# The feed-forward part of a fused attention and mixture kernel on one core: its order written out by hand, the conversion of its weights changed

## The chip, the cores and the metric

The kernel runs on one core of a Trainium2 chip. The time is device time in microseconds for one execution. The engines are PE (TensorE; PEld is its loading of weights), DVE (VectorE), ACT (ScalarE), POOL (GpSimd) and SP, which here issues the DMAs. Each runs its own instructions in its own order and waits for others by semaphores.

## What is computed

Attention with a top-32 mask (4 batches, 8 heads, 576 positions), a soft mixture of 8 experts over its result, and a feed-forward layer over the 2304 tokens. The part that this document is on is the last:

```python
def _moe2_ref(x, w_in, w_out):          # w_in 512 x 2048, w_out 2048 x 512
    h = x @ w_in
    pos, neg = h >= 1.0, h <= -1.0
    g = np.where(pos, h, np.where(neg, 0.0, (h + 1.0) ** 2 / 4.0))
    return (g @ w_out).astype(np.float32)
```

The weights `w_in` and `w_out` come as float64, as pairs of 32-bit words, and the kernel turns them into float32 with integer and float instructions: the absolute value of the high word read as a float, a lower bound, a shift left by 3, plus the scaled low word, and the sign put back.

## The kernel before

The attention and the mixture stand first (to about 575 us of the span) and aren't touched. Then SP streams the weights of the experts, four pieces of `w_in` that are converted earlier, and the 16 raw tiles of `w_out` (128 rows, 512 KB each) through a ring of 37 tiles of SBUF. The order of these loads is the list `worder`; `NRAW` of the raw tiles stand ahead of the pieces for `m_rest`.

x is a product itself, c times the experts' result, so the kernel first makes m = (experts' result) @ w_in, in four parts m4[0..3] of 512 columns: `m_first` makes the first, `m_rest` the other three in 24 matmuls, `m_spread(n)` brings each of these into the form that the h matmul needs. The tokens are cut into 6 blocks t of 384, the 2048 hidden columns into 16 pieces f of 128. A step is one pair (t, f): `emit_g` makes h = m4 . c in one matmul into PSUM, then relu and square on ACT, min and max in one DVE instruction (called min below), and cuts the result g into a high half gh (a cast) and a low half gl (a subtraction). `emit_o` multiplies: for each of three rows of 128 tokens gh . wh, gh . wl, gl . wh, nine matmuls that add into PSUM. wh and wl are the same two halves of the converted `w_out` piece f.

The steps run as (0,0), (1,0), (0,1), (1,1), ... through all f for t = 0 and 1, and then t = 2 to 5 one after the other. `wo_prep(f)` converts piece f by `narrow` (seven instructions: abs, scaled low word and sign on ACT, shift on DVE, max, add and multiplication by the sign on POOL) and cuts it; it does so `CLA` = 4 pieces ahead. h is made `GA` = 2 steps ahead. In this part the order on each engine isn't the order of the code: the scheduler of the framework sets it by its own estimates. The attention's order is written by hand (`ORDER`, under `tc.manual_schedule`).

Of the kernel before, what the change touches and what calls it, by code (L numbers as in the profile page):

```python
# [19 lines left out]
P = 128  # L20
# [10 lines left out]
NF = DFF // P  # L31
# [7 lines left out]
NTILE = NPAIR * 9  # L39
BIG = 2.0 ** 100  # L40
NEG = -1.0e30
CW = 512
NC1 = DFF // CW
NC2 = DM // CW
NWE = 0
NRAW = 2
NCV = NHP * NC1 + NWE
BLK = 384
NA = 13
# [4 lines left out]
MASK_POOL = ((0, 1), (2, 1), (4, 0))  # L54
NTR = 1
NV = 2
CLA = 4
ORDER = '''
Y30b z4b E00b Q30c A11c X21b P11b T40c S00a md M31b H1c A20c Y21b Q31c K20b c4c U01b E01b C00a
G00a K21b K30b c2c L4b S01a Q40c U11b N3b C01a R4c X31b Y31b A21c E10b S10a T00b T01b G01a B2b  # L60
# [8 lines left out]
GA = 2  # L69
NLAST = 3  # L70
# [3 lines left out]
def kernel_body(tc, qT, kT, vP, phi, w1, w2, w_in, w_out, out, fast, flag):  # L74
    nc = tc.nc
# [25 lines left out]
    two = cpool.tile([P, 1], F32, name="two")  # L101
# [736 lines left out]
    def m_first():  # L838
        ps = ps_m.tile([P, 512], F32, name="m_ps0", tag="m_ps")
        for c in range(NHP):  # L840
            nc.tensor.matmul(ps, so128[:, c].rearrange("p g s -> p (g s)"), wtile[(2, 0, c // 2)][c % 2],
                             start=(c == 0), stop=(c == NHP - 1))
        nc.scalar.copy(m4[0], ps)
        nc.vector.tensor_tensor(m4[0][64:], ps[64:], m4[0][64:].bitcast(F32), op=ALU.subtract)

    def m_rest():
        ps = ps_m.tile([P, 512], F32, name="m_ps1", tag="m_ps")
        for c in range(NHP):
            for n in range(1, NC1):
# [30 lines left out]
    pos = {}  # L880
    wo_t = {}

    def wo_prep(f):
        if f < NWE:
            wo = wtile[(3, 0, f // 2)][f % 2]
        else:
            tr = p_t.tile([P, 2, CW], I32, name="tr_l", tag="h1s", bufs=2)
            sg = p_t.tile([P, CW], BF16, name="sg_l", tag="sg_l", bufs=1)
            wo = narrow(wtile[(4, 0, f)], tr, sg, range(7))
        wh, wl = slot_tiles(w_slots[f], "whl", F32R)[1]  # L890
        nc.scalar.copy(wh, wo)
        nc.vector.tensor_tensor(wl, wo, wh.bitcast(F32), op=ALU.subtract)
        wo_t[f] = (wh, wl)

    def emit_g(s_):
        t, f = s_
        ph = ps_m.tile([P, 512], F32, name="h_ps", tag="m_ps")[:, :BLK]
        nc.tensor.matmul(ph, m4[f // 4][:, f % 4 * P:(f % 4 + 1) * P], cT[:, t * BLK:(t + 1) * BLK], start=True, stop=True)  # L898
        r, g = (x[:, :BLK] for x in ring_tile("g", g_slots, "rg", F32))
        nc.scalar.activation(r, ph, AF.Relu, bias=half, scale=0.5)  # L900
        nc.scalar.activation(r, r, AF.Square)  # L901
        nc.vector.scalar_tensor_tensor(g, ph, 1.0, r, op0=ALU.max, op1=ALU.min)  # L902
        gh, gl = (x[:, :BLK] for x in ring_tile("g", g_slots, "ghl", F32R))
# [19 lines left out]
    m_first()
    for k in range(CLA):
        wo_prep(k)
    for s_ in steps[:GA]:
        emit_g(s_)
    for i, s_ in enumerate(steps[:-NLAST]):
        t, f = s_
        if i == 1:  # L930
            mhl = m_rest()
        if t == 1 and f % 4 == 1 and f // 4 < NC1 - 1:
            m_spread(f // 4 + 1, *mhl)
        if t == 0 and f + CLA < NF:
            wo_prep(f + CLA)
        if i + GA < len(steps):
            emit_g(steps[i + GA])
        emit_o(t, f, range(NS))
    for s_ in steps[GA - NLAST:] if NLAST > GA else []:
        emit_g(s_)  # L940
    for n in range(NS):
        for s_ in steps[-NLAST:]:
            emit_o(*s_, [n])
# [65 lines left out]
```

## Time and profile before

| | us |
|---|---|
| median of 3 runs | 877.66 (876.0 to 878.2) |
| span of the profiled execution | 872.0 |
| feed-forward steps of t = 0 and 1 (with conversion) | 634.2 to about 722 |
| steps of t = 2 to 5 (no conversion) | about 722 to 865 |

The span is that of the instructions which the profiler recorded; the time of a run has a few microseconds around it. Busy time of an engine is the time in which it had an instruction under way, waits inside an instruction included. A row of the timeline gives start, duration, engine, line, operation, and what it writes and reads; a line number with L is that of the listing.

### The profile page before, as it was taken

The page shows a single profiled execution, that of the slowest core. Times are in us where ns is not written, and L with a number is a line of the kernel's source. Part 1 is how long each engine was busy: PE and PEld are TensorE (multiplying, and loading weights), DVE is VectorE, ACT ScalarE, POOL GpSimd, SP SyncE. Part 2 cuts the span into 40 slices and gives each one's busy share as a digit, 9 for nine tenths or more (in the row PEclk, how much of TensorE's full clock was granted, in tenths as well). Part 3 has the DMA queues.
Part 4 walks back from the last instruction along what each step waited for, and adds up shares of the span by engine and source line. Part 5 has one row for each costly group of instructions (what it writes and reads, how often), then busy time and mean ns, then how long its engine had stood idle before and what let it go on. Part 6 is the DMA issues. An engine that isn't in the chain of part 4 may idle for free.

```text
span 872.0 us, 17711 instructions
## 1 busy us (share of the span) xinstructions
PE 821.5 (94%) x5695; PEld 674.7 (77%) x5695; DVE 685.8 (79%) x3084; ACT 644.8 (74%) x1292; POOL 485.4 (56%) x494
## 2 busy tenths in 40 slices
PE   4889999999999999999999999799698899999996
PEld 3678989988989988988988988632266678888885
DVE  6999999988999989999989994103389995666663
ACT  5688999988998988998988987412578766545453
POOL 2577888877888877888877774100467740000000
PEclk9799999999999999999999999899799999999999
DMA  8453563553353353353452536699940001001001
GB/s 240 124 152 96 165 176 98 156 157 89 103 142 92 112 133 89 102 142 87 117 134 78 157 101 205 206 343 386 399 175 1 0 2 73 37 0 38 1 37 40
DMA packets 49461, 108.59 MB, mean 125 GB/s; under 512 B 8304, under 2 KB 8304, under 8 KB 49360
## 3 DMA queue, kind: packets, MB, share of 16 engines
q1 hardware_dynamic: 49040, 106.73, 40.2%
q8 instruction: 47, 0.77, 0.4%
q10 hardware_dynamic: 320, 0.66, 0.3%
q14 instruction: 54, 0.44, 0.2%
HBM read 70.70 MB, written 8.91 MB: 91 GB/s over the span
## 4 chain that ended last, share of the span: by engine, by line
PE 78%; DVE 10%; DMA 6%; ACT 3%; POOL 1%; issue 1%; ACTq 0%; POOLq 0%; SPq 0%; DVEq 0%
PE s_ps L311 20%; PE o_ps L916 17%; PE av_ps L485 14%; PE pt_ps L457 7%; PE s_ps L413 4%; PE av_ps L486 3%; PE rem_ps L230 3%; DMA w<-in_moe_w_dram 2%; DMA w<-in_moe_w_out_dram 2%; PE h L804 2%; DVE cand L338 2%; PE moe_ps L569 2%; DMA w<-cv_d 1%; PE h_ps L898 1%; PE xT_ps L534 1%
## 5 line engine op out<-in xcount | busy, mean ns | idle before, releaser
L311 PE MATMUL s_ps<-kh,q 128*128 128x288 f32 x640 | 208.1, 342 | 16.4 <-DVE q L266 9.0
L916 PE MATMUL o_ps<-whl,ghl 128*128 128x512 f32 x864 | 216.9, 395 | 5.0 <-DVE ghl L904 4.0
L916 PEld LDWEIGHTS o_ps<-whl,ghl 128*128 128x128 f32 x864 | 159.1, 188 | 44.7 <-DVE ghl L904 7.1
L445 POOL TENSOR_TENSOR ssb<-ssb,pen 128x576 f32<-128x576 f32 x141 | 180.4, 1284 | 18.3 <-ACT pen L442 15.8
L311 PE MATMUL s_ps<-kl,q 128*128 128x288 f32 x640 | 181.2, 299 | 0.0
L338 DVE MAX8 cand<-ssb 128x8 f32<-128x82 f32 (+1 forms) x1008 | 164.2, 228 | 5.0 <-ACT ssb L329 4.0
L311 PEld LDWEIGHTS s_ps<-kh,q 128*128 128x128 f32 x640 | 123.6, 193 | 34.7 <-DVE q L266 9.4
L485 PE MATMUL av_ps<-v_sb,ptb 128*128 128x65 f32 (+1 forms) x1280 | 147.1, 261 | 0.4 <-ACT xT L547 0.4
L485 PEld LDWEIGHTS av_ps<-v_sb,ptb 128*128 128x128 f32 (+1 forms) x1280 | 141.1, 181 | 5.2 <-issue 2.6
L311 PEld LDWEIGHTS s_ps<-kl,q 128*128 128x128 f32 x640 | 124.4, 194 | 0.3
L422 DVE MAX8 l<-s_ps 128x8 f32<-128x576 f32 x144 | 109.2, 758 | 18.3 <-PE s_ps L413 17.9
L442 ACT ACTIVATE pen<-ssb,kb 128x576 bf16<-128x576 f32 x141 | 110.3, 792 | 4.5 <-POOL kb L438 3.3
L329 ACT COPY ssb<-s_ps 128x576 f32<-128x576 f32 x144 | 91.1, 641 | 25.3 <-PE s_ps L311 21.8
L448 ACT ACTIVATE ssb<-ssb,nm 128x576 f32<-128x576 f32 x141 | 109.0, 785 | 0.6 <-POOL ssb L445 0.6
L900 ACT ACTIVATE rg<-h_ps,half 128x384 f32<-128x384 f32 x96 | 55.2, 579 | 71.0 <-PE h_ps L898 70.8
L396 POOL TENSOR_SCALAR mb<-ssb,top 128x576 bf16<-128x576 f32 x48 | 83.3, 1736 | 19.2 <-DVE top L345 9.2
L902 DVE SCALAR_TENSOR_TENSOR rg<-h_ps,rg 128x384 f32<-128x384 f32 x96 | 52.9, 554 | 47.4 <-ACT rg L901 47.1
L467 ACT COPY ptb<-pt_ps 128x512 f32<-128x512 f32 x144 | 82.4, 598 | 3.3 <-PE av_ps L485 3.3
L457 PE MATMUL pt_ps<-ident,ssb 128*128 128x128 f32 x576 | 84.3, 273 | 0.2
L398 DVE TENSOR_SCALAR_CACHE_REDUCE mb<-ssb,top 128x576 bf16<-128x576 f32 x96 | 75.8, 802 | 0.0
L345 DVE MAX8 top<-cand 128x8 f32<-128x56 f32 x432 | 73.5, 207 | 0.1
L457 PEld LDWEIGHTS pt_ps<-ident,ssb 128*128 128x128 f32 x576 | 68.7, 142 | 1.3 <-ACT ptb L467 0.8
(160 smaller groups left out, 1311.7 us busy)
## 6 DMA issues: line engine op xcount, KB each, us to landing
w<-in_moe_w_dram SPq DMA_DIRECT2D x60, 512.0 KB, 6.7
q<-qst SPq DMA_DIRECT2D x60, 160.0 KB, 3.1
kh<-kst SPq DMA_DIRECT2D x60, 144.0 KB, 2.5
kl<-kst SPq DMA_DIRECT2D x60, 144.0 KB, 2.9
x<-in_moe_w_in_dram SPq DMA_DIRECT2D x16, 512.0 KB, 3.9
w<-in_moe_w_out_dram SPq DMA_DIRECT2D x16, 512.0 KB, 9.3
v_sb<-in_v_dram SPq DMA_DIRECT2D x16, 325.0 KB, 2.9
raw_t<-in_q_dram SPq DMA_DIRECT2D x15, 320.0 KB, 3.7
```

The costliest lines, as they stand in the source:

```text
L311: nc.tensor.matmul(s[:, hf, :HS], a, w, start=(n == 0), stop=(n == len(terms) - 1), skip_group_check=True)
L329: nc.scalar.copy(st[u]["ssb"][:, j], st.pop((u, j))[:, :, :HS])
L338: nc.vector.max(st[u]["cand"][:, j, 8 * g:8 * g + 8], row(u, j)[:, S * g // NSEG:S * (g + 1) // NSEG])
L396: nc.gpsimd.tensor_scalar(st[u]["mb"][:, j], row(u, j), t_u, None, op0=ALU.is_ge)
L422: nc.vector.max(st[u]["l8"][:, j], st.pop((u, j))[:, :, :HS])
L442: nc.scalar.activation(pen, row(u, j), AF.Relu, bias=st[u]["kb"][:, j:j + 1], scale=-BIG)
L445: nc.gpsimd.tensor_tensor(row(u, j), row(u, j), st.pop((u, "pen", j)), op=ALU.subtract)
L448: nc.scalar.activation(row(u, j), row(u, j), AF.Exp, bias=st[u]["nm"][:, j:j + 1], scale=0.125)
L457: nc.tensor.transpose(pt[:, c, :], pr[:, c * P:(c + 1) * P], ident)
L467: nc.scalar.copy(ptb, st.pop((u, "pt", j)))
L485: nc.tensor.matmul(o, pj[:, c, sl], v_sb[:, 4 * jj + c, :], start=(c == 0), stop=False)
L916: nc.tensor.matmul(pos[t][n], a[:, sl], w, start=(f == 0 and k == 0), stop=(f == NF - 1 and k == 2))
```

## The change

1. The feed-forward part stands under `tc.manual_schedule`: each engine's order is that of the code, which `step(i)`, `emit_h`, `emit_g` and `prep(f, k)` write out. `prep` has five pieces: k=0 abs (ACT) and max (POOL), k=1 scaled low word (ACT, called identity below after its function), k=2 shift (DVE) and add (POOL), k=3 the sign, k=4 high half (ACT) and low half.
2. The sign is put back by one DVE instruction on integers, (high word and -2^31) or t, instead of a sign on ACT and a multiplication on POOL.
3. The low half of a weight piece is subtracted on POOL, for the first two on DVE as before.
4. For t=1, while there are pieces left to begin, the high half of g is cast on ACT instead of DVE.
5. `NRAW` is 4: two more raw tiles are loaded ahead of the pieces for `m_rest`. `m_rest` comes at step 3 instead of 1, its copies in two instead of three.

```diff
-NRAW = 2
+NRAW = 4
...
-    def wo_prep(f):
-        if f < NWE:
-            wo = wtile[(3, 0, f // 2)][f % 2]
-        else:
-            tr = p_t.tile([P, 2, CW], I32, name="tr_l", tag="h1s", bufs=2)
-            sg = p_t.tile([P, CW], BF16, name="sg_l", tag="sg_l", bufs=1)
-            wo = narrow(wtile[(4, 0, f)], tr, sg, range(7))
-        wh, wl = slot_tiles(w_slots[f], "whl", F32R)[1]
-        nc.scalar.copy(wh, wo)
-        nc.vector.tensor_tensor(wl, wo, wh.bitcast(F32), op=ALU.subtract)
-        wo_t[f] = (wh, wl)
...
+    def prep(f, k, last=None):
+        if f >= NF:
+            return
+        x64 = wtile[(4, 0, f)]
+        hf = x64[:, :, 1].bitcast(F32)
...
+        t, r = preps[f][:, 0], preps[f][:, 1]
+        tf = t.bitcast(F32)
+        if k == 0:
+            nc.scalar.activation(tf, hf, AF.Abs)
+            nc.gpsimd.tensor_scalar(tf, tf, 2.0 ** -15, None, op0=ALU.max)
+        elif k == 1:
+            nc.scalar.activation(r.bitcast(F32), x64[:, :, 0].bitcast(U32), AF.Identity, bias=two, scale=2.0 ** -51)
+        elif k == 2:
+            nc.vector.tensor_scalar(t, t, 3, None, op0=ALU.logical_shift_left)
+            nc.gpsimd.tensor_tensor(t, t, r, op=ALU.add)
+        elif k == 3:
+            nc.vector.scalar_tensor_tensor(t, x64[:, :, 1], SIGN, t, op0=ALU.bitwise_and, op1=ALU.bitwise_or)
+        else:
+            wh, wl = wo_t[f] = slot_tiles(w_slots[f], "whl", F32R)[1]
+            nc.scalar.copy(wh, tf)
+            (last or nc.gpsimd).tensor_tensor(wl, tf, wh.bitcast(F32), op=ALU.subtract)
+            del preps[f]
...
-        nc.vector.tensor_copy(gh, g)
+        if on_act:
+            nc.scalar.copy(gh, g)
+        else:
+            nc.vector.tensor_copy(gh, g)
         nc.vector.tensor_tensor(gl, g, gh.bitcast(F32), op=ALU.subtract)
...
+    def step(i):
+        t, f = steps[i]
+        nxt = steps[i + GA] if i + GA < len(steps) else None
+        if i == 3:
+            mhl.extend(m_rest())
+        if t == 1 and f % 4 == 2 and f // 4 < NC1 - 1:
+            m_spread(f // 4 + 1, *mhl)
+        if t == 0:
+            prep(f + 2, 3)
+        if nxt:
+            emit_h(nxt)
+        if t == 0:
+            prep(f + 2, 4)
+            prep(f + 3, 2)
+        elif t == 1:
+            prep(f + 4, 0)
+        if nxt:
+            emit_g(nxt, t == 1 and f + 4 < NF)
+        if t == 1:
+            prep(f + 4, 1)
+        emit_o(t, f, range(NS))
```

What stands on the engines now is shown for one pair of steps, that of f = 6; in both kernels `w_80` and `w_81` are the raw tiles of f = 8 and 9, `tr_l_10088` and `tr_l_10134` (before: `tr_l_10086` and `tr_l_10135`) the tiles in which they are converted.

DVE before, from the shift of f=8 on: `rg` is g before the cut, `ghl` its halves, `whl` the halves of a weight piece.

```order
L221 TENSOR_SCALAR tr_l_10086<-tr_l_10086 128x512
L892 TENSOR_TENSOR whl_10047<-tr_l_10037,whl_10046 128x512
L902 SCALAR_TENSOR_TENSOR rg_10172<-h_ps_10170,rg_10172 128x384
L904 CAST ghl_10176<-rg_10172 128x384
L905 TENSOR_TENSOR ghl_10176<-rg_10172,ghl_10176 128x384
L902 SCALAR_TENSOR_TENSOR rg_10202<-h_ps_10200,rg_10202 128x384
L892 TENSOR_TENSOR whl_10096<-tr_l_10086,whl_10095 128x512
```

DVE now, from the and-or of f=8 to that of f=9:

```order
L905 SCALAR_TENSOR_TENSOR tr_l_10088<-w_80_9513,tr_l_10088 128x512
L919 SCALAR_TENSOR_TENSOR rg_10153<-h_ps_10151,rg_10153 128x384
L902 TENSOR_SCALAR tr_l_10134<-tr_l_10134 128x512
L928 CAST ghl_10163<-rg_10153 128x384
L929 TENSOR_TENSOR ghl_10163<-rg_10153,ghl_10163 128x384
L919 SCALAR_TENSOR_TENSOR rg_10181<-h_ps_10179,rg_10181 128x384
L929 TENSOR_TENSOR ghl_10188<-rg_10181,ghl_10188 128x384
L905 SCALAR_TENSOR_TENSOR tr_l_10134<-w_81_9515,tr_l_10134 128x512
```

The low half of the weights (L892) is gone from DVE, one cast of the two as well; the and-or has come, and every pair has the same seven rows.

POOL before, from the max of f=8 on, which the scheduler mixed with the piece ahead of it:

```order
L219 TENSOR_SCALAR tr_l_10086<-tr_l_10086 128x512
L225 TENSOR_TENSOR tr_l_10037<-tr_l_10037,sg_l_10038 128x512
L223 TENSOR_TENSOR tr_l_10086<-tr_l_10086 128x512
L225 TENSOR_TENSOR tr_l_10086<-tr_l_10086,sg_l_10087 128x512
L219 TENSOR_SCALAR tr_l_10135<-tr_l_10135 128x512
```

POOL now, the same stretch:

```order
L898 TENSOR_SCALAR tr_l_10088<-tr_l_10088 128x512
L909 TENSOR_TENSOR whl_10111<-tr_l_10042,whl_10111 128x512
L903 TENSOR_TENSOR tr_l_10088<-tr_l_10088 128x512
L898 TENSOR_SCALAR tr_l_10134<-tr_l_10134 128x512
L909 TENSOR_TENSOR whl_10158<-tr_l_10088,whl_10157 128x512
L903 TENSOR_TENSOR tr_l_10134<-tr_l_10134 128x512
```

The multiplications (L225) are gone, the low halves (L909) have come, each between the max of the next piece and that piece's add.

ACT before, from the abs of f=8 to that of f=9:

```order
L213 ACTIVATE tr_l_10086<-w_80_9513 128x512
L215 ACTIVATE tr_l_10086<-w_80_9513,two_93 128x512
L901 ACTIVATE rg_10150<-rg_10150 128x384
L866 CAST m4_2_9398<-m_ps2_10166 128x512
L900 ACTIVATE rg_10172<-h_ps_10170,half_75 128x384
L891 CAST whl_10046<-tr_l_10037 128x512
L217 ACTIVATE sg_l_10087<-w_80_9513 128x512
L900 ACTIVATE rg_10202<-h_ps_10200,half_75 128x384
L901 ACTIVATE rg_10172<-rg_10172 128x384
L213 ACTIVATE tr_l_10135<-w_81_9515 128x512
```

ACT now, the same stretch:

```order
L897 ACTIVATE tr_l_10088<-w_80_9513 128x512
L926 CAST ghl_10091<-rg_10084 128x384
L900 ACTIVATE tr_l_10088<-w_80_9513,two_93 128x512
L917 ACTIVATE rg_10107<-h_ps_10105,half_75 128x384
L918 ACTIVATE rg_10107<-rg_10107 128x384
L908 CAST whl_10111<-tr_l_10042 128x512
L917 ACTIVATE rg_10130<-h_ps_10128,half_75 128x384
L918 ACTIVATE rg_10130<-rg_10130 128x384
L897 ACTIVATE tr_l_10134<-w_81_9515 128x512
```

The cast of gh for t=1 (L926) stands between the abs and the identity; behind it come the identity and the relu and square of the next pair's t=0. The sign (L217) is gone.

## Rows read from the trace of the kernel before

**Rows 1.** The page of the profile: its first line, and the busy time of each engine (us, share of the span, instructions).

```profile
span 872.0 us, 17711 instructions
...
PE 821.5 (94%) x5695; PEld 674.7 (77%) x5695; DVE 685.8 (79%) x3084; ACT 644.8 (74%) x1292; POOL 485.4 (56%) x494
```

**Rows 2.** The feed-forward part by stretches: busy time of each engine in each stretch (us, instructions), mean granted TensorE clock, mean share of the DMA engines, GB/s.

```profile
core 0: us, PE busy (x) PEld busy (x) DVE busy (x) ACT busy (x) POOL busy (x), PEclk, DMA share, GB/s
622.00:634.00 12.00, 7.26 (x27) 1.93 (x27) 3.83 (x8) 5.79 (x11) 6.06 (x5) 0.57 1.03 408
634.00:640.00 6.00, 5.30 (x23) 3.59 (x20) 4.78 (x8) 5.47 (x10) 3.35 (x3) 1.00 1.02 408
640.00:660.00 20.00, 18.34 (x75) 13.27 (x75) 18.59 (x30) 16.02 (x30) 14.10 (x11) 1.00 0.08 31
660.00:680.00 20.00, 18.09 (x73) 12.60 (x72) 18.66 (x30) 15.67 (x30) 15.90 (x12) 1.00 0.00 1
720.00:740.00 20.00, 20.00 (x91) 16.67 (x90) 12.50 (x27) 11.80 (x23) 0.00 (x0) 1.00 0.21 79
```

**Rows 3.** DVE in order of time at two places of the same part: start, duration (us), engine, line, operation, tiles, shapes.

```profile
636.29 0.75 DVE L904 CAST ghl<-rg 128x384 fp32r<-128x384 f32 x1
...
657.39 0.68 DVE L892 TENSOR_TENSOR whl<-tr_l,whl 128x512 fp32r<-128x512 f32 x1
658.10 0.56 DVE L902 SCALAR_TENSOR_TENSOR rg<-h_ps,rg 128x384 f32<-128x384 f32 x1
658.70 0.76 DVE L904 CAST ghl<-rg 128x384 fp32r<-128x384 f32 x1
659.49 1.41 DVE L905 TENSOR_TENSOR ghl<-rg,ghl 128x384 fp32r<-128x384 f32 x1
...
661.47 0.36 DVE L904 CAST ghl<-rg 128x384 fp32r<-128x384 f32 x1
661.87 0.56 DVE L905 TENSOR_TENSOR ghl<-rg,ghl 128x384 fp32r<-128x384 f32 x1
662.34 0.68 DVE L892 TENSOR_TENSOR whl<-tr_l,whl 128x512 fp32r<-128x512 f32 x1
```

**Rows 4.** POOL in order of time at the same two places (the last brackets, where there are some, give idle time before the instruction and what ended it).

```profile
636.22 1.49 POOL L219 TENSOR_SCALAR tr_l<-tr_l 128x512 f32<-128x512 f32 x1 [3.54 <-ACT tr_l L213]
...
657.63 1.60 POOL L223 TENSOR_TENSOR tr_l<-tr_l 128x512 int32<-128x512 int32 x1 [0.61 <-DVE tr_l L221]
659.31 1.18 POOL L225 TENSOR_TENSOR tr_l<-tr_l,sg_l 128x512 f32<-128x512 f32 x1
660.45 1.85 POOL L219 TENSOR_SCALAR tr_l<-tr_l 128x512 f32<-128x512 f32 x1
```

**Rows 5.** The tile of the conversion, tr_l, over the whole feed-forward part: shortest, median and longest duration in ns of the instructions of each line, first and last start.

```profile
L219 POOL TENSOR_SCALAR tr_l<-tr_l x16: 1484/1550/1967, 616.8 to 706.2; 128x512 f32<-128x512 f32 x16
L221 DVE TENSOR_SCALAR tr_l<-tr_l x16: 414/426/1482, 618.3 to 708.6; 128x512 int32<-128x512 int32 x16
L223 POOL TENSOR_TENSOR tr_l<-tr_l x16: 1255/1294/1802, 620.1 to 709.1; 128x512 int32<-128x512 int32 x16
L225 POOL TENSOR_TENSOR tr_l<-tr_l,sg_l x16: 1152/1170/1663, 623.0 to 710.5; 128x512 f32<-128x512 f32 x16
L892 DVE TENSOR_TENSOR whl<-tr_l,whl x16: 675/685/1655, 624.8 to 714.0; 128x512 fp32r<-128x512 f32 x16
```

**Rows 6.** PE in order of time, ahead of the stage and at its end (consecutive like instructions are one row, with their count).

```profile
616.77 3.70 PE L841 MATMUL m_ps<-w,so 128*128 128x512 f32 x8 [0.71 <-DVE so L835]
...
627.98 6.29 PE L850 MATMUL m_ps<-w,so 128*32 128x512 f32 x24
634.20 2.33 PE L916 MATMUL o_ps<-whl,ghl 128*128 128x512 f32 x9
...
719.88 4.29 PE L916 MATMUL o_ps<-whl,ghl 128*128 128x512 f32 x18
```

**Rows 7.** ACT in order of time at two places of the feed-forward part.

```profile
649.11 0.58 ACT L900 ACTIVATE rg<-h_ps,half 128x384 f32<-128x384 f32 x1
649.72 0.53 ACT L901 ACTIVATE rg<-rg 128x384 f32<-128x384 f32 x1
...
659.00 0.76 ACT L215 ACTIVATE tr_l<-w,two 128x512 f32<-128x512 uint32 x1
659.66 0.51 ACT L901 ACTIVATE rg<-rg 128x384 f32<-128x384 f32 x1
660.08 0.56 ACT L900 ACTIVATE rg<-h_ps,half 128x384 f32<-128x384 f32 x1
660.54 0.60 ACT L891 CAST whl<-tr_l 128x512 fp32r<-128x512 f32 x1
661.05 0.67 ACT L217 ACTIVATE sg_l<-w 128x512 bf16<-128x512 f32 x1
```

**Rows 8.** POOL's groups of instructions by line and shape, over the whole execution: count, busy us, mean ns of one, idle time before them.

```profile
L286 POOL TENSOR_TENSOR qst<-raw_t,qst 128x640 fp32r<-128x640 f32 x15 | 23.2, 1546 | 9.3 <-ACT qst L282 9.3
...
L284 POOL TENSOR_TENSOR kst<-raw_t,kst 128x576 fp32r<-128x576 f32 x15 | 21.2, 1411 | 0.0
```

**Rows 9.** ACT and then DVE at the first m, ahead of the stage.

```profile
620.51 0.59 ACT L843 CAST m<-m_ps 128x512 fp32r<-128x512 f32 x1 [1.33 <-PE m_ps L841]
...
621.66 0.69 DVE L844 TENSOR_TENSOR m<-m_ps,m 64x512 fp32r<-64x512 f32 x1
```

More of the change, by code (lines that the diff above doesn't have):

```diff
@@ L41 @@
 NEG = -1.0e30
+SIGN = -2 ** 31
 CW = 512
@@ L56 @@
 NV = 2
-CLA = 4
 ORDER = '''
@@ L853, in m_rest @@
         mh, ml = mhl[:, 0], mhl[:, 1]
-        for n in range(1, NC1):
-            rows = slice(32 * n, 32 * n + 32)
+        for rows in (slice(32, 64), slice(64, P)):
             nc.scalar.copy(mh[rows], ps[rows])
@@ L881, in kernel_body, with emit_h @@
     wo_t = {}
-    def wo_prep(f):
-        if f < NWE:
-            wo = wtile[(3, 0, f // 2)][f % 2]
-        else:
-            tr = p_t.tile([P, 2, CW], I32, name="tr_l", tag="h1s", bufs=2)
-            sg = p_t.tile([P, CW], BF16, name="sg_l", tag="sg_l", bufs=1)
-            wo = narrow(wtile[(4, 0, f)], tr, sg, range(7))
-        wh, wl = slot_tiles(w_slots[f], "whl", F32R)[1]
-        nc.scalar.copy(wh, wo)
-        nc.vector.tensor_tensor(wl, wo, wh.bitcast(F32), op=ALU.subtract)
-        wo_t[f] = (wh, wl)
-    def emit_g(s_):
+    preps = {}
+    def prep(f, k, last=None):
[4 more added lines that the diff above has]
+        if k == 0:
+            if f % 3 == 2:
+                preps[f] = slot_tiles(mix_slots[0], "tr_l", I32)[0]
+            else:
+                preps[f] = p_t.tile([P, 2, CW], I32, name="tr_l", tag="h1s", bufs=2)
+        t, r = preps[f][:, 0], preps[f][:, 1]
+        tf = t.bitcast(F32)
+        if k == 0:
+            nc.scalar.activation(tf, hf, AF.Abs)
[7 more added lines that the diff above has]
+            nc.vector.scalar_tensor_tensor(t, x64[:, :, 1], SIGN, t, op0=ALU.bitwise_and, op1=ALU.bitwise_or)
+        else:
+            wh, wl = wo_t[f] = slot_tiles(w_slots[f], "whl", F32R)[1]
+            nc.scalar.copy(wh, tf)
+            (last or nc.gpsimd).tensor_tensor(wl, tf, wh.bitcast(F32), op=ALU.subtract)
+            del preps[f]
+    def emit_h(s_):
         t, f = s_
@@ L902, in emit_g @@
         nc.vector.scalar_tensor_tensor(g, ph, 1.0, r, op0=ALU.max, op1=ALU.min)
+        gs[s_] = g
+    def emit_g(s_, on_act=False):
+        g = gs.pop(s_)
         gh, gl = (x[:, :BLK] for x in ring_tile("g", g_slots, "ghl", F32R))
-        nc.vector.tensor_copy(gh, g)
+        if on_act:
+            nc.scalar.copy(gh, g)
+        else:
+            nc.vector.tensor_copy(gh, g)
         nc.vector.tensor_tensor(gl, g, gh.bitcast(F32), op=ALU.subtract)
@@ L921, in emit_o @@
                 nc.sync.dma_start(out[t * BLK + n * P:t * BLK + (n + 1) * P, :], o)
[L923 to L932, printed above, removed]
-            m_spread(f // 4 + 1, *mhl)
[L934 to L937, printed above, removed]
-        emit_o(t, f, range(NS))
[L939 to L943, printed above, removed]
+    def step(i):
[4 more added lines that the diff above has]
+        if t == 1 and f % 4 == 2 and f // 4 < NC1 - 1:
+            m_spread(f // 4 + 1, *mhl)
+        if t == 0:
[11 more added lines that the diff above has]
+            prep(f + 4, 1)
+        emit_o(t, f, range(NS))
+    mhl = []
+    with tc.manual_schedule(engines={ET.PE, ET.Activation, ET.DVE, ET.Pool}):
+        prep(0, 0)
+        prep(0, 1)
+        prep(0, 2)
+        prep(1, 0)
+        prep(1, 1)
+        m_first()
+        emit_h(steps[0])
+        prep(0, 3)
+        prep(0, 4, nc.vector)
+        prep(1, 2)
+        emit_g(steps[0])
+        prep(2, 0)
+        prep(2, 1)
+        emit_h(steps[1])
+        emit_g(steps[1])
+        prep(1, 3)
+        prep(1, 4, nc.vector)
+        prep(2, 2)
+        prep(3, 0)
+        prep(3, 1)
+        for i in range(len(steps) - NLAST):
+            step(i)
+        for s_ in steps[GA - NLAST:]:
+            emit_h(s_)
+            emit_g(s_)
+        for n in range(NS):
+            for s_ in steps[-NLAST:]:
+                emit_o(*s_, [n])
     tail.close()
```

## Prediction

> **What bounds the kernel now.** I read the page's busy shares first: PE 94% of the span, DVE 79%, ACT 74%, POOL 56% [rows 1]. The diff touches only the feed-forward part, so the shares of that stretch count [rows 2]. Each of the 96 steps there is one h matmul and nine o matmuls, ten on PE. From 720 to 740 us, where no weights are converted any more, PE issues 91 in 20 us: 9.1 steps, 2.2 us each. From 640 to 680 it issues 148, four of them spreading m: 14.4 steps, 2.78 us each, or 5.6 us for a pair (t=0 and t=1 of one f) where PE alone needs 4.48. PE looks busy at 18.3 and 18.1 of 20 us only because the records overlap. DVE is at 18.6 of 20: it sets the pace.
>
> DVE's own work doesn't fill that. Undelayed, its cast takes 0.36 us and its subtraction 0.56; beside POOL they take 0.76 and 1.41 [rows 3]. The cast from 658.70 ends at 659.46, which is the end of POOL's add (657.63 + 1.60 = 659.23), less 0.12, plus 0.35. The subtraction from 659.49 ends at 660.90: the end of POOL's multiplication (660.49), less 0.12, plus 0.54 [rows 3, 4]. So one waits for the whole of the other. It goes the other way too: that add itself took 0.35 over its 1.25 because the low-half subtraction on DVE (657.39 to 658.07) was under way [rows 3 to 5]. POOL's multiplication began 0.15 before the end of that cast without delay, so DVE lets go some 0.14 before its recorded end; its own next instruction starts some 0.08 before it (661.87, 662.34). DVE's min, which reads PSUM, takes its 0.56 beside POOL's add and isn't held. POOL's max holds DVE only at first: the cast at 661.47, 1.02 us after the max began, takes its usual 0.36 [rows 3, 4]. A cast that starts 0.07 after a max (636.29) takes 0.75, so it was let in 0.47 after the max's start [rows 3, 4]; I count the first 0.48 us of a max as holding.
>
> Ahead of the stage, PE idles after its first m (620.47), the granted clock falls (0.57 on average from 622 to 634, that is, 1.2 GHz for most of it), and 24 matmuls for the other three parts of m take 6.29 us before the first o at 634.20 [rows 2, 6]. The 32 steps of t=0 and 1 end half way through PE's block of 18 from 719.88, 4.29 long: 722.0 [rows 6]. From there on before and after are alike.
>
> **The change, part by part.** Per f ACT loses the sign (0.67) and gains one cast; DVE loses one cast (0.36) and the low half (0.68) and gains the and-or; POOL swaps its multiplication (1.15) for the low half [rows 3, 5, 7]. By busy time alone all would fit: ACT 4.2, DVE 3.3, POOL 4.0 us in a pair, under PE's 4.48. What decides is the order, which is now fixed, with the waits between DVE and POOL in it.
>
> Prices. The and-or isn't in this trace: it has 512 elements and two SBUF inputs as the low half on DVE has, so 0.68, next one 0.60 later; bounds 0.41 (the shift) and 1.66 (that low half with a wait) [rows 3, 5]. The low half on POOL: f32 subtractions there take 1.411 for 576 and 1.546 for 640 elements [rows 8], by the line through both 1.27 for 512; bounds 1.15 and 1.41. The cast on ACT: the square of 384 elements takes 0.51 and the next starts 0.42 later; I take the same. ACT's relu to its own square is 0.61, the identity to the next 0.66, the high half 0.60 [rows 7]. POOL's add is 1.26, its max 1.48 when undisturbed [rows 5].
>
> One pair, time 0 at the start of the and-or (f+2). ACT's order is relu, square, high half, relu, square, abs, cast, identity; DVE's and-or, min, shift, cast, sub, min, sub; POOL's low half, add, max.
> - ACT's cast of the pair before stood at -1.03 (derived at the end of this list). Behind it come identity (+0.42), relu (+0.66), at 0.05, and square, at 0.65, done at 1.16. High half 1.06 to 1.67.
> - DVE: min at 1.20; shift at 1.68, letting go at 1.95.
> - POOL: low half ready at 1.71, after the shift lets go 1.97 to 3.24. DVE's cast, due at 2.0, waits to 3.12 and ends 3.46.
> - POOL: add, ready, gets in behind the cast (lets go 3.32): 3.34 to 4.60. DVE's sub, due at 3.5, waits to 4.48 and ends 5.03.
> - POOL: max 4.91 to 6.39. DVE: min 4.96 to 5.51, not held.
> - ACT: cast at 5.55, which had to wait for that min with identity and the next pair's relu and square queued behind it. DVE: last sub 6.10, next and-or 6.58 (5.55 + 1.03).
>
> So the pair takes 6.58 us, a ring with no slack: ACT 2.2 (cast, identity, relu, square), DVE's min, shift, cast, sub, min, and in the middle the two whole POOL instructions, some 2.2 us of waiting. It was 5.6.
>
> Sum. The head: ACT copies m from 620.51 to 621.10, DVE subtracts (0.69) to 621.83 [rows 9], then the first h, relu and square to 623.35, min to 623.94, and-or to 624.55, high half on ACT to 625.2, low half, here still on DVE, to 625.93, shift, cast to 626.5: o starts at 626.6 instead of 634.2, at 1.2 GHz as before. Its third matmul needs gl, held by POOL's add for f=1 until 628.1. DVE's and-or and low half for f=1 follow at 629.5 to 631.55, the shift for f=2 lets POOL's add begin at 631.94, and the first pair's and-or (f=2), behind that add and the first part of a max, comes at 633.65. Pair 0 has no identity chain yet: 5.98, to 639.6. Pair 1 contains m's 24 matmuls, which wait for o(0,1) (gl at 638.1), and ACT waits for them: 3.4 us at full clock, 6.8 at half, so their end lies at 643.1 to 648; taking 645, then two copies and subs in turn (2.6 us), relu, square, min: and-or at 649.7. Pairs 2 to 11: 10 x 6.58 = 65.8, to 715.5. The last four pairs lose the max, then the add and the low half, and have DVE's own cast back; the low half of f=15 ends 9.1 us in, DVE's gl for f=14 at 9.5, and PE runs four steps behind that: 18.3 in all, to 733.8. Against 722.0: **+11.8 us**. The profiled span is 872.0 [rows 1]; the median of the three runs, 877.66, lies 5.7 above it, which I carry over: 883.8 + 5.7 = 889.5.
>
> At nothing: the twelve loads for m's other parts come behind two more raw tiles, 1 MB at 408 GB/s [rows 2], 2.6 us later; they were used from 627.98 on [rows 6] and are now used after 639, so the first three steps cover it; without that cover it would cost the 2.6. The raw tiles 2 and 3 are there sooner, which ends no wait (the trace has none there). Two copies for m instead of three save 0.6 once, counted above.
>
> The SBUF — State Buffer page of the Trainium skill (Who interferes with whom) has a GpSimd instruction hold the shared pair for its whole length, the max too; [rows 4] show a max that lets the cast through after a third. By the page, the first and-or of the loop would wait to the end of the max ahead, 0.9 us more once: 890.4 instead of 889.5.
>
> **Rivals.**
> - *The moved work simply relieves DVE* (faster). If POOL's and DVE's instructions hardly met, the pair would be cast 2.0, sub 2.4, min 2.9, ACT's cast 3.45: 4.48 us, PE's own pace. PE's work from 626.6 on, half speed until about 633, ends near 708: 14 us less, 863 to 864. For it: ACT and DVE do lose 0.3 and 0.7 us a pair. Against: every cast and sub of [rows 3] that met an add or a multiplication waited for it. It decides if both waits in the ring vanish; the break-even pair is 5.5. Chance 0.20. Perfetto Trace Analysis in the Trainium skill (Optimizing Scalar/DVE Operations) says that offloading a saturated DVE may make sense, and that between DVE and GPSIMD it might not help as they share a port; the trace so far speaks for the second half.
> - *One of the two waits* (about the same). If the cast gets in ahead of the low half (it comes 0.3 later by my times), POOL's low half ends at 3.47, sub at 3.9, and the pair is 5.45: 11 x 1.13 less, 877. Chance 0.14.
> - *PE's clock falls in the loop* (slower still). PE would idle 2.1 of 6.58 us; before, it idled about 1 of 5.6 at full clock [rows 2]. At 1.2 GHz two steps take 9 us: 24 more, about 913. Chance 0.04.
> - *The and-or is dear or is held* (1.6 us): only what exceeds the 0.6 that it has until the square is done counts, 0.4 a pair, 5 in all: inside my range.
>
> **How the numbers follow.** My forecast has 0.62: 889, its own range 881 to 898 (POOL's low half 1.15 to 1.41 is -1.5 to +1.5, the and-or up to +5, m's matmuls +-2.5, the cast on ACT +-0.1 a pair). The whole range: the fast rival reaches 862, the slow one 913. Leaving out the lower half of the fast one (0.10), the clock (0.04) and a little of the upper edge gives 864 to 897. The bound of a measurable change is 0.3%, 2.6 us. Faster: 0.20 + 0.06 of the one-wait case = 0.26; same: 0.08 of it and 0.02 of mine, 0.10; slower 0.64.
>
> **What would show it.** In the loop's stretch: steps 3.2 to 3.3 us apart (right) or 2.24 (the fast rival); DVE's casts and subs at about 1.45 us on average for t=0 and 0.55 for t=1's sub; ACT idle before its cast on DVE's min; the first o near 626.6; m's matmuls near 640. Wrong would be: casts at 0.36 beside POOL's low half, or the and-or far from 0.68, or a head that starts later than 627.

## The result and the profile after

The changed kernel takes **890.01 us** (median of 4, 887.38 to 890.48) where the kernel before takes 876.83 beside it: ratio **1.0131, 95% interval 1.0094 to 1.0168**. A second set gave 889.35 against 877.36, 1.0135 (1.0109 to 1.0161). It is slower, by 12 to 13 us; 889 was forecast.

The page of the changed kernel, beside [rows 1], and the same part by stretches, beside [rows 2] (columns as there):

```profile
span 888.6 us, 17683 instructions
...
PE 831.8 (94%) x5695; PEld 680.4 (77%) x5695; DVE 691.5 (78%) x3073; ACT 643.1 (72%) x1287; POOL 487.2 (55%) x492
```

```profile
660.00:680.00 20.00, 16.71 (x63) 12.27 (x62) 16.23 (x21) 13.06 (x26) 14.12 (x10) 0.91 0.00 0
680.00:700.00 20.00, 16.10 (x66) 11.29 (x65) 16.52 (x22) 13.66 (x27) 14.13 (x10) 1.00 0.00 1
700.00:720.00 20.00, 16.04 (x65) 11.29 (x64) 16.56 (x23) 13.66 (x27) 13.83 (x10) 1.00 0.00 0
```

The shares of the whole say nothing: they have hardly moved. In the loop PE now issues 63 to 66 matmuls in 20 us where it issued about 74, and **no** engine is busier than before: DVE 16.5 of 20 us instead of 18.6, ACT 13.7 instead of 15.7 to 16.0, POOL 14 instead of 14 to 16. None of them is the bound. So the time is in a chain through several engines, and one pair shows it. First DVE, then POOL, then ACT, in order of time:

```profile
667.39 0.68 DVE L905 SCALAR_TENSOR_TENSOR tr_l<-w,tr_l 128x512 int32<-128x512 int32 x1
668.62 0.56 DVE L919 SCALAR_TENSOR_TENSOR rg<-h_ps,rg 128x384 f32<-128x384 f32 x1 [0.55 <-ACT rg L918]
669.09 0.42 DVE L902 TENSOR_SCALAR tr_l<-tr_l 128x512 int32<-128x512 int32 x1
669.42 1.45 DVE L928 CAST ghl<-rg 128x384 fp32r<-128x384 f32 x1
670.90 1.53 DVE L929 TENSOR_TENSOR ghl<-rg,ghl 128x384 fp32r<-128x384 f32 x1
672.36 0.55 DVE L919 SCALAR_TENSOR_TENSOR rg<-h_ps,rg 128x384 f32<-128x384 f32 x1
673.49 0.56 DVE L929 TENSOR_TENSOR ghl<-rg,ghl 128x384 fp32r<-128x384 f32 x1 [0.58 <-ACT ghl L926]
673.96 0.69 DVE L905 SCALAR_TENSOR_TENSOR tr_l<-w,tr_l 128x512 int32<-128x512 int32 x1
```

```profile
669.18 1.47 POOL L909 TENSOR_TENSOR whl<-tr_l,whl 128x512 fp32r<-128x512 f32 x1 [1.98 <-ACT whl L908]
670.61 1.41 POOL L903 TENSOR_TENSOR tr_l<-tr_l 128x512 int32<-128x512 int32 x1
671.99 1.80 POOL L898 TENSOR_SCALAR tr_l<-tr_l 128x512 f32<-128x512 f32 x1
```

```profile
668.49 0.61 ACT L908 CAST whl<-tr_l 128x512 fp32r<-128x512 f32 x1
...
672.94 0.51 ACT L926 CAST ghl<-rg 128x384 fp32r<-128x384 f32 x1 [2.25 <-DVE rg L919]
673.36 0.76 ACT L900 ACTIVATE tr_l<-w,two 128x512 f32<-128x512 uint32 x1
674.03 0.56 ACT L917 ACTIVATE rg<-h_ps,half 128x384 f32<-128x384 f32 x1
674.62 0.53 ACT L918 ACTIVATE rg<-rg 128x384 f32<-128x384 f32 x1
```

Read it as the ring of the forecast. ACT sits 2.25 us idle ahead of its cast until DVE's min is done (672.91), then does cast, identity, relu and square (to 675.15); DVE's min waits for that square, 0.55 us in the pair shown (668.62). Behind the min come shift, a cast of 1.45 us that needs 0.35 (it ends at 670.87; POOL's low half at 670.65) and a subtraction of 1.53 that needs 0.56 (POOL's add ends at 672.02, less 0.12, plus 0.55 is 672.45, against a measured 672.43). Then the min, and round again: 673.96 - 667.39 = 6.57 us. Ten such pairs stand between the third pair's and-or and the thirteenth's, 65.6 us, 6.56 each.

In the tables below "stage" is the trace's distance from the first m matmul to the first o matmul of t=2, and "pair" the mean of those ten distances. Before, the stage was 721.98 - 616.77 = 105.2 us (the first of these from the single matmul's record; [rows 6] give it as half a block). A pair was 5.55: that kernel has no and-or and its order changes from pair to pair, so it is taken from the first o matmuls of t=0, f=4 and f=14 (657.40 and 712.92). After, it is 738.21 - 623.13 = **115.1 us, 9.9 more** (PE, beside [rows 6]; the second row is t=2's first nine):

```profile
623.13 3.70 PE L841 MATMUL m_ps<-w,so 128*128 128x512 f32 x8 [0.71 <-DVE so L835]
...
738.21 2.25 PE L940 MATMUL o_ps<-whl,ghl 128*128 128x512 f32 x9
```


The spans differ by 16.6, though. Another 6.4 us (623.13 - 616.77) lie ahead of the stage, in code that the change doesn't touch: from 569 to 623 us the granted clock was 1.00 in the kernel before and 0.88 in the changed one (first row: before; second: after).

```profile
569.00:623.00 54.00, 48.99 (x317) 16.12 (x309) 12.35 (x26) 14.24 (x28) 5.45 (x4) 1.00 1.04 384
```

```profile
569.00:623.00 54.00, 49.71 (x309) 15.77 (x309) 9.97 (x24) 12.16 (x26) 0.62 (x1) 0.88 1.02 371
```

Whether the change does that (two more raw tiles are loaded there) was open; the first two experiments are about it.

### The profile page after: what moved, and what is told of

Read it like the earlier page. It is cut to its first block, busy times and chain, and to the rows that moved or that the text cites. A ratio compares the mean times of both kernels' runs of the same rounds, so it can differ in the third digit from the quotient of the medians.

```text
span 888.6 us, 17683 instructions
## 1 busy us (share of the span) xinstructions
PE 831.8 (94%) x5695; PEld 680.4 (77%) x5695; DVE 691.5 (78%) x3073; ACT 643.1 (72%) x1287; POOL 487.2 (55%) x492
## 4 chain that ended last, share of the span: by engine, by line
PE 77%; DVE 11%; ACT 5%; DMA 4%; issue 1%; POOL 0%; SPq 0%; ACTq 0%; POOLq 0%; DVEq 0%
PE s_ps L311 20%; PE o_ps L940 16%; PE av_ps L485 14%; PE pt_ps L457 7%; PE s_ps L413 4%; PE av_ps L486 3%; DMA w<-in_moe_w_dram 3%; PE rem_ps L230 3%; DVE ghl L929 2%; DVE ghl L928 2%; PE moe_ps L569 2%; DVE rg L919 2%; DVE cand L338 1%; PE h_ps L915 1%; PE xT_ps L534 1%
## 5 line engine op out<-in xcount | busy, mean ns | idle before, releaser
L940 PE MATMUL o_ps<-whl,ghl 128*128 128x512 f32 x864 | 223.1, 401 | 15.4 <-DVE ghl L928 7.7
L940 PEld LDWEIGHTS o_ps<-whl,ghl 128*128 128x128 f32 x864 | 162.0, 191 | 57.0 <-DVE ghl L929 13.8
L445 POOL TENSOR_TENSOR ssb<-ssb,pen 128x576 f32<-128x576 f32 x141 | 180.4, 1284 | 19.0 <-ACT pen L442 16.6
L929 DVE TENSOR_TENSOR ghl<-rg,ghl 128x384 fp32r<-128x384 f32 x96 | 68.1, 709 | 9.9 <-ACT ghl L926 7.0
```

The source lines that it names most:

```text
L445: nc.gpsimd.tensor_tensor(row(u, j), row(u, j), st.pop((u, "pen", j)), op=ALU.subtract)
```

## The experiments

All are the changed kernel with one thing altered, but for again, which is that kernel itself, and best1 and best1_pool, where the text says what differs. "Ratio" is against the kernel before, run beside it on the same chip; the sets come from three chips, so kernels of different sets are better compared by it than by their medians. Stage and pair are those of one profiled execution each.

| kernel | stage us | pair us | median us | ratio (95%) |
|---|---|---|---|---|
| before | 105.2 | 5.55 | 876.1 to 877.4 | 1 |
| changed | 115.1 | 6.56 | 890.0 | 1.0131 (1.0094 to 1.0168) |
| again | 115.1 | 6.57 | 889.4 | 1.0135 (1.0109 to 1.0161) |
| nraw2 | 117.2 | 6.56 | 889.2 | 1.0148 (1.0115 to 1.0182) |
| ident_first | 101.5 | 5.26 | 874.6 | 0.9965 (0.9941 to 0.9988) |
| cast_dve | 103.1 | 5.50 | 875.3 | 0.9983 (0.9964 to 1.0001) |
| low_dve | 110.9 | 6.13 | 884.6 | 1.0107 (1.0070 to 1.0143) |
| dbl_low | 115.7 | 6.58 | 890.0 | 1.0152 (1.0120 to 1.0184) |
| no_max | 114.9 | 6.58 | 886.4 | 1.0126 (1.0097 to 1.0154) |
| high_late | 105.6 | 5.58 | 879.9 | 1.0027 (1.0008 to 1.0045) |
| best1 | 95.2 | 4.80 | 869.2 | 0.9925 (0.9899 to 0.9952) |
| best1_pool | 101.9 | 5.52 | 875.3 | 0.9971 (0.9955 to 0.9988) |
| free | 107.3 | 5.18 | 879.9 | 1.0024 (1.0005 to 1.0042) |

**again, nraw2: is the 6.4 us ahead of the stage the change's?** nraw2 is one number:

```
-NRAW = 4
+NRAW = 2
```

> The changed kernel itself once more. Its profiled execution stands 6.4 us later than that of the kernel before already at the first m matmul (623.2 against 616.8), ahead of the changed part. Theory A (the two extra raw tiles are loaded in a stretch that the loads bound, and PE gets its weights later): the 6.4 us are there again, within 1 us. Theory B (the stretches of half clock fall in other places from execution to execution): the first m lies anywhere from 617 to 624, and moves with the granted clock of 560 to 620. Both: the loop's pairs 6.5 to 6.6 us apart, 887 to 891 us.

> Two raw tiles ahead instead of four, the rest as changed. Theory A: the first m lies 5 to 6 us earlier than with four, and the time falls by as much, to 884 or 885. Theory B: no change of the time beyond what the clock's place makes of it, 887 to 891, and the loads for m's other parts 2.6 us earlier (two tiles of 0.5 MB at 408 GB/s) with nobody waiting for them.

The first m matmul stood at 623.0 in again and at 618.4 in nraw2, which alone would look like theory A; but the times are the same (889.4, 889.2), and the kernels with four tiles that come below had it anywhere from 617.8 (cast_dve) to 622.6 (high_late), with the same code up to there. It goes with the granted clock, as B has it. The mean clock from 548 to 616 us was 0.95 in before and cast_dve (first m at 616.8 and 617.8), 0.92 in nraw2 (618.4) and in low_dve, no_max, best1, best1_pool and free (619.1 to 619.5), 0.87 in the changed kernel and again (623.1, 623.0), 0.85 in ident_first, dbl_low and high_late (622.1 to 622.6). At the same clock, four tiles stand 0.7 to 1.1 us behind two (617.8 against 616.8, 619.1 to 619.5 against 618.4): that much can be theory A's, the rest is B. 18 executions of the kernel before on the chip of these runs had spans from 871.9 to 877.9 us at mean clocks between 0.984 and 0.972; its profile, 872.0, is one of the quickest.

nraw2 also shows a small price that I had at nothing: with two tiles ahead ACT waits for the third one (first row), which makes the distance from the first and-or to the second 0.9 us longer. The other 1.2 us by which its stage is longer are not the tiles': they lie in pair 1, where seven o matmuls ahead of m's ran into a stretch at a granted clock of 0.50 and took 3.08 us (second row) instead of 1.88 in the changed kernel.

```profile
628.26 0.68 ACT L897 ACTIVATE tr_l<-w 128x512 f32<-128x512 f32 x1 [1.33 <-DMA w<-in_moe_w_out_dram]
...
639.74 3.08 PE L940 MATMUL o_ps<-whl,ghl 128*128 128x512 f32 x7 [0.76 <-DVE ghl L929]
```

**ident_first, cast_dve: is ACT in the ring?** ident_first moves one instruction on ACT; cast_dve gives DVE back the cast of t=1.

```
 # ident_first
+        if t == 1:
+            prep(f + 4, 1)
         if nxt:
             emit_g(nxt, t == 1 and f + 4 < NF)
-        if t == 1:
-            prep(f + 4, 1)
 # cast_dve
-            emit_g(nxt, t == 1 and f + 4 < NF)
+            emit_g(nxt)
```

> ACT's identity of f+4 ahead of its cast of t=1 instead of behind it, nothing else. The ring theory (ACT cast, identity, relu, square, DVE min, shift, POOL low half, DVE cast, POOL add, DVE sub, min, and again the cast, with no slack): the identity falls out of the ring, so each pair is shorter by its 0.66 us, 5.9 instead of 6.56; over 12 pairs 8 us, about 882. The rival, that DVE and POOL together are simply full (their work that holds the other out, and the order on ACT doesn't matter): no change, 890.

> The cast of t=1 back on DVE, as before the change. The ring theory: ACT is out of the ring; what is left is DVE's own row with the two POOL instructions in it: and-or 0.60, min 0.50, shift 0.27, low half 1.27, cast 0.34, add 1.26, sub 0.55, min 0.50, cast 0.36, sub 0.55, less some 0.3 where one lets go before its end: 5.9 us a pair, 0.65 less, about 882, although DVE has more to do. The rival that DVE and POOL together are full: 0.36 more a pair, 6.9, about 894.

The rival falls: with the same work in another order the pair is 1.3 us shorter, and with more work on DVE 1.06. But both gains are 1.6 to 2 times what I expected. The rows of ident_first tell why (DVE, then POOL):

```profile
674.22 1.10 DVE L905 SCALAR_TENSOR_TENSOR tr_l<-w,tr_l 128x512 int32<-128x512 int32 x1
675.24 0.54 DVE L919 SCALAR_TENSOR_TENSOR rg<-h_ps,rg 128x384 f32<-128x384 f32 x1
675.71 0.41 DVE L902 TENSOR_SCALAR tr_l<-tr_l 128x512 int32<-128x512 int32 x1
676.04 0.35 DVE L928 CAST ghl<-rg 128x384 fp32r<-128x384 f32 x1
676.42 1.53 DVE L929 TENSOR_TENSOR ghl<-rg,ghl 128x384 fp32r<-128x384 f32 x1
```

```profile
673.82 1.82 POOL L898 TENSOR_SCALAR tr_l<-tr_l 128x512 f32<-128x512 f32 x1
676.05 1.49 POOL L909 TENSOR_TENSOR whl<-tr_l,whl 128x512 fp32r<-128x512 f32 x1 [0.41 <-ACT whl L908]
```

The cast takes 0.35: it started 0.01 us **ahead** of POOL's low half and isn't held. One whole wait is gone with the identity. Why it is ahead shows when both are counted from the end of the and-or, which both follow. The low half comes 0.73 us behind it here (675.32 to 676.05) and the cast 0.72. In the changed kernel's loop (and-or ended at 668.07) the low half came 1.11 behind, since ACT still had the square to do, and the cast 1.35, since DVE's min waited for that same square. So ACT's square, which comes later by the identity ahead of it, held the cast up by 0.63 us and the low half by 0.38; without that the cast is just in front. cast_dve has it in every pair too (DVE, then POOL):

```profile
672.08 0.35 DVE L928 CAST ghl<-rg 128x384 fp32r<-128x384 f32 x1
```

```profile
672.10 1.49 POOL L909 TENSOR_TENSOR whl<-tr_l,whl 128x512 fp32r<-128x512 f32 x1 [0.87 <-ACT whl L908]
```

So neither run tells what ACT's instructions alone are worth: each took ACT's chain away from DVE's min, and one of the two waits fell out with it. That the whole max does not hold is seen beside this: the and-or ended at 675.32, while the max ran to 675.64.

**high_late: is it really who is ready first?** If so, a later low half must make the kernel faster:

```
         nc.scalar.activation(r, ph, AF.Relu, bias=half, scale=0.5)
+        if between:
+            between()
         nc.scalar.activation(r, r, AF.Square)
```

For t=1 `between` issues the high half, the low half and the add, which are taken out of the step of t=0.

> The changed kernel with ACT's high half issued behind the relu of t=1 instead of ahead of it (some 0.5 us later), and with it POOL's low half; all else, POOL's and DVE's own orders included, as it is. In the changed kernel POOL's low half becomes ready at 669.15 and DVE's cast behind the shift comes at 669.42, so the cast waits for the whole low half. The theory that who is ready first gets in first: with the low half ready at about 669.65 the cast is ahead of it and takes 0.36, the low half then holds the sub, which would have been held by the add in any case, and one of the two waits falls out of the ring: 5.4 to 5.6 us a pair in place of 6.56, 875 to 879, although the converted word comes later. The rival, that the low half stands in the ring wherever it is: 0 to 0.5 us more a pair, 890 to 896.

```profile
672.95 0.35 DVE L934 CAST ghl<-rg 128x384 fp32r<-128x384 f32 x1
673.34 1.53 DVE L935 TENSOR_TENSOR ghl<-rg,ghl 128x384 fp32r<-128x384 f32 x1
```

```profile
673.17 1.28 POOL L913 TENSOR_TENSOR whl<-tr_l,whl 128x512 fp32r<-128x512 f32 x1 [0.83 <-ACT whl L912]
674.42 1.60 POOL L907 TENSOR_TENSOR tr_l<-tr_l 128x512 int32<-128x512 int32 x1
```

The cast at 672.95 is ahead of the low half at 673.17, the subtraction waits for the low half, and the add meets the min. Most pairs are 5.2 to 5.5 us; the two in which ACT also copies a part of m are 6.3. The stage is 9.5 us shorter for half a microsecond of delay. The time, 879.9, is 1 us above what I gave.

**dbl_low, no_max: do the holds add up?**

```
 # dbl_low
-            (last or nc.gpsimd).tensor_tensor(wl, tf, wh.bitcast(F32), op=ALU.subtract)
+            for _ in range(1 if last else 2):
+                (last or nc.gpsimd).tensor_tensor(wl, tf, wh.bitcast(F32), op=ALU.subtract)
 # no_max
-            nc.gpsimd.tensor_scalar(tf, tf, 2.0 ** -15, None, op0=ALU.max)
```

> POOL does the low half twice, one directly behind the other (the second writes the same words again). The ring theory, with who is ready first gets in first: DVE's cast waits for the first as before and gets in ahead of the second, DVE's sub then waits for the second in place of the add (both 1.3 us long), and the add lies beside the min, which is not held; POOL has room for it (4.0 of 6.56 us): 0 to 0.3 us a pair, 890 to 894. The rival, that what POOL and DVE hold each other out with adds up: 1.27 us more a pair, 905 to 909.

> POOL's max left out (words below 2 to the power -15 then come out otherwise). The ring theory: the max lies beside DVE's min and the wait for ACT's cast, so nothing in the ring waits for it: no change, 6.5 to 6.6 us a pair, 888 to 891. The rival, that the held time adds up: the 0.48 us that a max holds go, 6.1 a pair, 884; that POOL's busy time counts: 1.5 less, 872.

The pairs are as the ring theory has them: 1.3 us more on POOL in every pair cost 0.02 us, and 1.5 less gained nothing (stage 114.9; the profiled execution is 4 us shorter because its first m stands at 619.2 instead of 623.1). The median of no_max, 886.4, lies below the 888 I gave at least; against the kernel before, which was quicker in that set too, it is 1.0126, as the changed kernel's 1.0131. In dbl_low the cast gets in behind the first of POOL's two low halves, the subtraction behind the second, and the add falls beside the min:

```profile
668.41 1.45 DVE L929 CAST ghl<-rg 128x384 fp32r<-128x384 f32 x1
669.89 1.52 DVE L930 TENSOR_TENSOR ghl<-rg,ghl 128x384 fp32r<-128x384 f32 x1
671.34 0.54 DVE L920 SCALAR_TENSOR_TENSOR rg<-h_ps,rg 128x384 f32<-128x384 f32 x1
```

```profile
668.23 2.77 POOL L910 TENSOR_TENSOR whl<-tr_l,whl 128x512 fp32r<-128x512 f32 x2 [0.40 <-ACT whl L908]
670.96 1.59 POOL L903 TENSOR_TENSOR tr_l<-tr_l 128x512 int32<-128x512 int32 x1
```

**low_dve: the low half of every f on DVE.**

```
-            (last or nc.gpsimd).tensor_tensor(wl, tf, wh.bitcast(F32), op=ALU.subtract)
+            nc.vector.tensor_tensor(wl, tf, wh.bitcast(F32), op=ALU.subtract)
```

> The low half of every f on DVE (the changed kernel has the first two there), in its place between the first min and the shift; nothing else. One of the two POOL instructions that hold DVE is gone, and DVE has 0.60 us more. The ring theory, time 0 at the and-or: high half done at 1.67, low half 1.7 to 2.3, shift 2.3 to 2.6, POOL's add 2.65 to 3.9, DVE's cast held until 3.8, the max behind it holds the sub until 4.5, sub to 5.05, min 5.5, and ACT's cast stands where it stood: 6.3 to 6.6 us a pair, 886 to 890. The rival, that each of the two waits is worth what it lasts: 1.1 us less and 0.6 more, 6.0 to 6.1 a pair, about 884.

6.13 a pair and 884.6: the rival's numbers. My working had the cast wait for the add and the subtraction for the max; in the trace the cast (677.99, 0.35) is ahead of the add (678.22), and only the subtraction waits. So one wait of 1.1 us less, 0.6 us of work more, in the same ring: ACT still idles 1.80 us ahead of its cast.

**best1: an order with few meetings.** The cast of t=0 on ACT instead of that of t=1, the identity (of f+3) and the abs early, POOL's max ahead of its add, the low half on DVE (that line is low_dve's; the lines taken out of `step` are not shown).

```
+            emit_h(nxt, lambda: prep(f + 3, 1))
+            prep(f + 4, 0)
+            prep(f + 3, 2)
+            prep(f + 2, 4)
+            emit_g(nxt, f + 2 < NF)
+        elif nxt:
             emit_h(nxt)
...
+            emit_g(nxt)
```

> An order in which DVE waits for POOL as little as can be: low half on DVE; the cast of t=0, and not that of t=1, on ACT; identity (of f+3) between relu and square of t=0, abs ahead of the high half; POOL max, then add. In a pair DVE has and-or 0.60, min 0.48, shift 0.35, low half 0.60, sub 0.50, min 0.48, cast 0.36, sub 0.50: 3.9 us, with POOL's add beside the second min and its max beside the first. The ring theory: what is left of waits is 0.6 to 1.0 us, 4.6 to 4.9 a pair (PE alone 4.48), 1.7 to 2.0 less over 12 pairs: 866 to 870. The rival, that another wait takes the place of those two: 5.3 or more a pair, 875 and more.

869.2 us, 0.9925 (0.9899 to 0.9952) of the kernel before: faster than both. The loop is now at PE's own pace: its steps are 2.22 to 2.27 us apart, but for those that also spread m (3.4).

```profile
660.00:680.00 20.00, 19.79 (x87) 15.87 (x87) 18.20 (x35) 18.34 (x37) 13.14 (x9) 1.00 0.00 1
```

**best1_pool: the low half back on POOL in that order; free: the scheduler's order.**

```
 # best1_pool, against best1
-            nc.vector.tensor_tensor(wl, tf, wh.bitcast(F32), op=ALU.subtract)
+            (last or nc.gpsimd).tensor_tensor(wl, tf, wh.bitcast(F32), op=ALU.subtract)
 # free, against the changed kernel: the last part
-    with tc.manual_schedule(engines={ET.PE, ET.Activation, ET.DVE, ET.Pool}):
+    with ExitStack():
```

> The order of best1, with the low half on GpSimd again (behind the add), as in the changed kernel; nothing else. This is one edit of the change in an order that is otherwise good. The ring theory: POOL then has max, add and low half in a pair, 4.0 us, all but the max's later part holding DVE; DVE's own held work is 2.4 us, so a pair can't be below 0.48 + 1.27 + 1.26 + 2.4 = 5.4 less what one lets go early (0.12 to 0.14 each, some 0.5): 4.9 to 5.6 us against 4.46, 5 to 13 us more than best1 (869.2): 874 to 882. The rival, that the low half relieves DVE on POOL when the order is good: 4.46 as in best1, 868 to 870.

> The changed kernel's operations with the feed-forward part left to the scheduler that orders the kernel before, instead of the order written out. In the order that comes out, ACT's casts of t=1 often stand between relu and square of later steps, or right behind the high half, and two weight words are converted at a time in the later pairs. If the fixed order alone makes the change slow: a pair of 4.9 to 5.6 us, 868 to 878. If the low half on POOL makes it slow in any order: 6 us a pair and more, 884 and more.

best1_pool does on each engine nearly what the changed kernel does (only the casts on ACT are those of the other t) and is some 14 us faster by the ratios, 13.2 in the stage. With ident_first, where nothing but the order differs, that shows that it is the order which made the change slow. Within best1's order the low half on POOL costs some 4 us against DVE by the ratios (0.9971 against 0.9925), 6.7 in the stage, so that edit is a loss in a good order too. free lies outside the times of both its cases: its mean pair, 5.18, is that of the first, but its time misses that one's 878. Its first o comes 13.5 us after the first m instead of 10.0, and its pairs lie 1.1 to 7.9 us apart, since it converts two weight words at a time, so it says little of the order. No run has the and-or, or the later place of `m_rest`, without the rest of the change.

## Why the prediction was right, step by step

- **The ring**: 6.58 us forecast, 6.56 measured. DVE's cast 1.46 (measured 1.45), sub 1.53 (1.53), second sub 0.55 (0.56), and-or 0.68 (0.68), ACT's cast 0.51 (0.51), ACT idle on DVE's min (2.25 us). POOL's low half undelayed was 1.27; it took 1.28 and 1.30 where nothing was in its way (high_late). That ACT is in the ring, its 2.25 us idle on DVE's min and the 0.55 that DVE's min waits for ACT's square show; that the order decides, and not the work, ident_first; that the held times don't add up, dbl_low and no_max.
- **The head**: first o 9.8 us after the first m forecast, 10.0 measured; the loop's first and-or 16.9 and 16.7. The granted clock was 0.50 from 633 to 639, 1.2 GHz, as assumed.
- **Pair 0**: 5.98 forecast, 5.24 measured; the step that failed is the same that fails in the gains of the experiments. I gave the cast 0.3 us behind the low half's being ready. Here it was 0.02 ahead, so it wasn't held: in pair 0 DVE's min doesn't wait for ACT yet, as in ident_first. One pair later the min stands behind ACT's square, the cast is 0.18 behind, and 0.25 in the loop's pairs from then on. again and nraw2 do the same (DVE, then POOL):

```profile
639.82 1.09 DVE L905 SCALAR_TENSOR_TENSOR tr_l<-w,tr_l 128x512 int32<-128x512 int32 x1 [1.46 <-POOL tr_l L903]
...
641.63 0.35 DVE L928 CAST ghl<-rg 128x384 fp32r<-128x384 f32 x1
...
647.09 1.46 DVE L928 CAST ghl<-rg 128x384 fp32r<-128x384 f32 x1
```

```profile
639.76 1.48 POOL L898 TENSOR_SCALAR tr_l<-tr_l 128x512 f32<-128x512 f32 x1
641.65 1.47 POOL L909 TENSOR_TENSOR whl<-tr_l,whl 128x512 fp32r<-128x512 f32 x1 [0.41 <-ACT whl L908]
...
646.91 1.42 POOL L909 TENSOR_TENSOR whl<-tr_l,whl 128x512 fp32r<-128x512 f32 x1 [0.42 <-ACT whl L908]
```

- **The max** lets DVE in after its first part (0.48 us forecast): the and-or at 639.82 beside a max from 639.76 ended at 640.91, so it was let in at 640.23, 0.47 after the max's start. By the SBUF — State Buffer page of the Trainium skill (Who interferes with whom) it would have waited to the max's end, 641.24; the trace does not agree.
- **m's matmuls** ended 25.9 us after the first m (645.40 + 3.63, at full clock) where 28.2 was taken, and the third pair's and-or came at 31.1 instead of 32.9. Ten pairs (65.8 forecast, 65.6 measured) and the **last four** (18.3 and 18.3) were right.
- **The sum**: the stage grew by 9.9 instead of 11.8; of the 1.9, 0.7 are pair 0, 0.9 m's matmuls, 0.2 the head and 0.2 the ten pairs. That the total came within half a microsecond of the working's 889.5 is partly luck: the 5.7 us that I carried from the span to the median are 2 around the span (888.6 against 890.4) and 3.7 of an uncommonly quick profiled execution of before. The second set puts the difference of the medians at 12.0. So the medians differ by 2 to 3 us more than the stages; about 1 of that can be the two tiles ahead of the stage, which the sum had at nothing, and the rest isn't settled.
- **At nothing**: the later loads for m cost nothing, as said. That the two raw tiles end no wait held for the order before, not for this one: without them the head pays 0.9 us.
- **The rivals.** *Moved work relieves DVE* (863) came in no run: even in best1_pool the low half on POOL cost. Perfetto Trace Analysis in the Trainium skill (Optimizing Scalar/DVE Operations) warns that offloading between DVE and GPSIMD might not help; the 6.7 us between the stages of best1 and best1_pool agree. *One of the two waits* (5.45 a pair, 877) was nearer than its 0.14 says: pair 0 ran so, and with half a microsecond's delay of the high half so did nearly the whole loop (5.2 to 5.5, 879.9). *PE's clock falls in the loop*: 0.91 in one stretch of 20 us, 1.00 in the next two. *The and-or is dear*: its median is that of the low half on DVE.

## What to carry to other kernels

When no engine in a stretch is busier than before and the stretch is still longer, look in one period for the instruction that takes several times its undelayed length and the engine that idles on it, and write the ring down, including what is queued behind its waiting instruction. With two engines that hold each other out, the count of meetings that the ring waits for sets the pace, not their work: 1.3 us more work beside an instruction that isn't held was free, and an instruction made ready half a microsecond later took a wait away. Before an order is fixed by hand, compute for each such meeting who is ready first and by how much; count both from the last instruction that both wait for, with the queue that each stands in; a margin of 0.3 us is none.

## What was not expected of the hardware

- Hundredths of a microsecond decided which of two engines got in, and the same way in each execution: in the changed kernel, again and nraw2 DVE's cast starts 0.01 to 0.02 us ahead of POOL's low half in pair 0 and takes 0.35, and 0.18, then 0.25 behind in the pairs from then on and takes 1.45. Pair 0 took 5.24 us, a pair of the loop 6.56. Whether one order could run on in either way isn't shown: in pair 0 ACT's queue doesn't reach DVE's min yet.
- Executions with the same code there (but for the two raw tiles more) reach the first m matmul anywhere from 616.8 to 623.1 us, with a granted clock from 569 to 623 us of 1.00 in the profile of before and 0.88 in that of the changed kernel. That is half of what this change costs, so a stage is better compared from its own first instruction than by spans. A half-clock stretch inside the stage still counts: one made nraw2's 1.2 us longer.
